# Head of a routed feed-forward kernel: VectorE's turned squares put behind the choice of the group in front

## The chip, the cores and the metric

One core of a Trainium2 chip runs the whole program. The metric is the device time of one execution in microseconds (us); lower is better. The engines' short names are those of the profile: PE is TensorE (PEld its weight loads), DVE is VectorE, ACT is ScalarE, POOL is GpSimd, and SP is SyncE, which here issues nearly all plain DMAs. The "q" of SPq marks an instruction that an engine's sequencer runs, such as the issue of a DMA.

## What is computed

A causal convolution of seven taps per head is followed by a feed-forward layer in which each row goes to one of eight experts, by the largest logit.

```python
# x (8, 3584, 192); weight (8, 7): softmax over the taps, heads of 24 columns
out = einsum('hk,bskhg->bshg', w, x_unf)          # convolution; then 28672 rows of 192
logits = x @ w_gate + modality_bias[modality_id]  # 8 experts
e_idx = argmax(logits, axis=1)
gate_w = softmax(logits)[arange(N), e_idx]
for e in range(8):
    h = maximum(x[e_idx == e] @ w1[e], 0)         # w1 (8, 192, 1024)
    out[e_idx == e] = gate_w * (h @ w2[e])        # w2 (8, 1024, 192)
```

## The kernel before

The rows go through in 19 groups (`QUADS_OF_GROUP` = 1, 1, 2, 1, 1, 2, then 4 each; the code counts them from 0). A quad is four tiles of 120 rows of four batches. The code's group g goes through these steps.

1. SP loads its input, one DMA of 384 KB for each quad (`load`, L317 and L320). The first eleven groups load into two long-lived tiles, so the load of a later group waits until the convolutions of an earlier one have read the place. In the trace these loads are `x<-in_x_dram`.
2. `convolve_pair` (L365, PE) makes the convolution of two heads in PSUM (`cv`); ACT, and DVE for a few, copies it to the tile `y` (L368, L370).
3. `turn` (L385, DVE) turns the 32x32 squares of `y` for one quad into the tile `turned`: one STREAM_TRANSPOSE of 128x768.
4. `gate` (L405, PE) multiplies `turned` with the gate's weights into `gt`: six matmuls for each quad, which the trace shows as twelve.
5. `logits` (L412, L415, DVE) turns `gt` back and adds the bias. `choose` (L428 to L446, DVE with one exponential on ACT) takes the largest logit (`top`, `ex`, `rk`, `first`) and the one-hot choice `oh` (L441).
6. `place` (L463, L466 on PE; L468 to L487 on DVE) counts the rows of each expert and gives the row numbers `idx` (L487). The running count `carry` goes on to the next group.
7. `send` (L251, POOL) scatters the tiles to their experts' rows in DRAM, one indirect DMA for each tile.

The first four groups (`FIRST` = 4: four, four, eight and four tiles, 20 scatters) make chunk 0. Once its rows are counted, `table(0)` (L634 to L698, DVE) works out which expert each slot of rows belongs to. From the table SP issues slot 0's weights (L736, L738, L741) and, behind the landing of chunk 0's scatters, the slot's rows (`raw<-routed_rows`, L771) and `tags`. The code's group 6, of four quads, still runs before slot 0: its four squares are turned, gated and chosen, and behind its gates stand the products `tps` that turn slot 0's rows (L802 to L804). Then comes the long part of the program: matmuls L835, L855 and L859 over 38 slots, into which the later groups are mixed.

Within the head (everything ahead of the first L835) nothing fixes the order by hand: a scheduler places each engine's instructions once, when the program is built, and each engine then runs its own queue in that order. `tc.issue_after(ins)` tells the scheduler to put what is recorded under it behind `ins`. SP's queue is such a list too, so an instruction of SP that waits holds back every DMA behind it.

Of the kernel before, what the change touches and what calls it, by code (L numbers as in the profile page):

```python
# [14 lines left out]
ALU = mybir.AluOpType  # L15
# [34 lines left out]
def conv_then_routed_ffn(ctx, tc, x, weight, modality, w_gate, mod_bias, w1, w2, out):  # L50
    nc = tc.nc
    NB, S, D = x.shape
# [11 lines left out]
    OVER = 2  # L64
    Q = 32
    NK = D // Q
    W = D + OVER
# [21 lines left out]
    turns, state = {}, {}  # L89

    def ring(pool, n, shape, dtype, name, tag=None):

        tag = tag or name
        k = turns[tag] = turns.get(tag, -1) + 1
        return pool.tile(shape, dtype, name=name, tag=f"{tag}_{k % n}", bufs=1)
# [25 lines left out]
    def warm(n):  # L121
# [9 lines left out]
        out=tri, in_=ones, compare_op=ALU.is_gt, fill=0.0, base=0,  # L131
# [145 lines left out]
    class Group:  # L277
# [103 lines left out]
        def turn(self, q):  # L381

            t0 = self.b0 + 4 * q % NB
            self.turned = ring(gp, 2, [P, NK, 4, Q], F32, "turned")
            nc.vector.transpose(out=self.turned.rearrange("p k t c -> p t k c"),  # L385
                                in_=self.ys[4 * q // NB][:, t0:t0 + 4, OVER:W].rearrange("p t (k c) -> p t k c", c=Q))

        def part_turned(self, q):

# [29 lines left out]
        def choose(self):  # L419

            n = self.tiles
            lg = self.lg

            def per_tile(ap):
                return ap.unsqueeze(2).broadcast_to([MB, n, E])

            top = rt.tile([MB, NT], F32, name="top")[:, 0:n]
            nc.vector.tensor_reduce(out=top, in_=lg, axis=AX.X, op=ALU.max)  # L428
            ex = rt.tile([MB, NT, E], F32, name="ex", bufs=1)[:, 0:n]
            nc.vector.tensor_tensor(out=ex, in0=lg, in1=per_tile(top), op=ALU.subtract)  # L430
            self.oh_and_none = rt.tile([MB, NT, E], BF16, name="oh")[:, 0:n + (self.g < SUMMED)]
            self.oh = self.oh_and_none[:, 0:n]
            if self.g < SUMMED:
                nc.vector.memset(self.oh_and_none[:, n], 0.0)
            rk = rt.tile([MB, NT, E], F32, name="rk", bufs=1)[:, 0:n]
            nc.vector.scalar_tensor_tensor(out=rk, in0=ex, scalar=0.0, in1=ramp.unsqueeze(1).broadcast_to([MB, n, E]),
                                           op0=ALU.is_equal, op1=ALU.mult)
            state["exp"] = nc.scalar.activation(out=lg, in_=ex, func=AF.Exp).ins
            first = rt.tile([MB, NT], F32, name="first")[:, 0:n]
            nc.vector.tensor_reduce(out=first, in_=rk, axis=AX.X, op=ALU.max)  # L440
            nc.vector.tensor_tensor(out=self.oh, in0=rk, in1=per_tile(first), op=ALU.is_equal)  # L441
            den = rt.tile([MB, NT], F32, name="den")[:, 0:n]
            nc.vector.tensor_reduce(out=den, in_=lg, axis=AX.X, op=ALU.add)
            nc.vector.tensor_scalar(out=den, in0=den, scalar1=1e-9, scalar2=None, op0=ALU.add)
            for i, y in enumerate(self.ys):
                nc.vector.reciprocal(out=y[0:MB, self.b0:self.b0 + self.nb, 0], in_=den[:, i * self.nb:(i + 1) * self.nb])  # L446
                with tc.issue_after(state["scatter"]) if "scatter" in state else nullcontext():
                    nc.gpsimd.iota(y.bitcast(I32)[0:MB, self.b0:self.b0 + self.nb, 1], pattern=[[S, self.nb]],
                                   base=self.b0 * S + (self.block + i) * MB - CUT + MB - 1,
                                   channel_multiplier=-1)  # L450
# [47 lines left out]
    FIRST = GROUPS_OF_CHUNK[0]  # L498
# [583 lines left out]
```

## Time and profile before

| | us |
|---|---|
| median of 3 runs | 1234.53 (1234.31 to 1235.81) |
| the profiled execution's own time | 1234.43 |
| its span, first to last instruction | 1232.6 |
| what lies around the span | 1.8 |
| PE busy in the span | 1211.1 (98%) |
| DVE busy | 967.9 (79%) |
| ACT busy | 723.3 (59%) |
| POOL busy | 528.7 (43%) |
| PE's first matmul of slot 0 (L835) | starts at 56.68 |

Times in the trace are counted from the span's start. A row of a timeline gives start, length, engine, line, operation, output and input; the brackets at its end give the engine's idle time just before, and what ended it. The chain of waits lists, in order of time, the pieces of work that led to the end.

### The profile page before, as it was taken

The numbers are of one execution on the slowest core, as the hardware profiler recorded it, in microseconds if no ns is written. First come the engines' busy times: TensorE is split into PE (matmuls) and PEld (weight loads), VectorE is DVE, ScalarE is ACT, GpSimd is POOL, SyncE is SP. The second block draws the span as 40 slices with busy tenths as digits, with TensorE's granted clock in tenths as the row PEclk, the third lists the DMA queues.
The fourth block names the chain that finished last, engine by engine and source line by source line (L and its number), as shares of the span: only waits on it lengthen the run. The fifth ranks groups of instructions, "written<-read, shape, count | busy, mean of one in ns | idle before, by whom it ended". The sixth has DMA issues, their size and how long they took to land.

```text
span 1232.6 us, 27980 instructions
## 1 busy us (share of the span) xinstructions
PE 1211.1 (98%) x9220; PEld 1196.6 (97%) x9220; DVE 967.9 (79%) x2455; ACT 723.3 (59%) x1588; POOL 528.7 (43%) x549
## 2 busy tenths in 40 slices
PE   9899999999999999999999999999999999999996
PEld 7799999999999999999999999999999999999995
DVE  6788986888788888788778887777766666787894
ACT  2366655565666556666655666555555555566773
POOL 7756564636344343545445344344352122112221
PEclk9999999999999999999999999999999999999998
DMA  8897563345544354345532554233262344943271
GB/s 222 221 224 211 122 179 77 77 116 142 134 88 111 84 125 110 72 107 142 143 63 57 109 121 126 53 71 61 73 158 56 81 106 106 258 112 94 42 191 38
DMA packets 308448, 144.29 MB, mean 117 GB/s; under 512 B 222922, under 2 KB 294930, under 8 KB 308293
## 3 DMA queue, kind: packets, MB, share of 16 engines
q1 hardware_dynamic: 284574, 97.83, 36.7%
q0 software_dynamic: 22752, 44.54, 11.6%
q8 instruction: 74, 1.21, 0.4%
q14 instruction: 81, 0.66, 0.2%
q10 hardware_dynamic: 967, 0.03, 0.0%
HBM read 116.58 MB, written 51.82 MB: 137 GB/s over the span
## 4 chain that ended last, share of the span: by engine, by line
PE 84%; DVE 6%; DMA 3%; issue 3%; ACT 1%; POOL 1%; SPq 0%; POOLq 0%; DVEq 0%; ACTq 0%
PE hps L835 39%; PE po L855 25%; PE po L859 12%; PE gt L405 3%; PE cv L349 3%; PE cv L365 2%; DMA routed_rows<-y,idx 1%; DVE hl L839 1%; DVE w1b L110 1%; DMA xr<-in_x_dram 1%; ACT lowp L871 1%; DVE xl L110 1%; DVE w2b L110 1%; POOL out_dram L874 0%; DVE sxs L822 0%
## 5 line engine op out<-in xcount | busy, mean ns | idle before, releaser
L855 PE MATMUL po<-w2b,hh 128*128 128x384 f32 x1824 | 556.3, 355 | 0.0
L835 PE MATMUL hps<-sxh,w1b 128*128 128x256 f32 x1824 | 482.0, 287 | 3.2 <-DVE hl L839 2.0
L839 DVE SCALAR_TENSOR_TENSOR hl<-hps,hh 128x512 fp32r<-128x512 f32 x456 | 312.0, 686 | 193.9 <-ACT hh L838 191.2
L838 ACT ACTIVATE hh<-hps 128x512 fp32r<-128x512 f32 x456 | 272.7, 598 | 324.6 <-PE hps L835 319.1
L859 PE MATMUL po<-w2b,hl 128*128 128x192 f32 x1824 | 443.4, 253 | 0.0
L874 POOL DMA_INDIRECT out_dram<-o,tags x228 | 236.5, 1037 | 382.5 <-DVE o L873 320.3
L251 POOL DMA_INDIRECT routed_rows<-y,idx x240 | 262.3, 1093 | 300.4 <-DVE hl L839 146.8
L835 PE MATMUL hps<-sxs,w1b 128*128 128x256 f32 x1824 | 363.5, 281 | 0.4 <-DVE sxs L822 0.4
L835 PEld LDWEIGHTS hps<-sxh,w1b 128*128 128x128 f32 x1824 | 344.8, 189 | 8.5 <-DVE hl L839 8.0
L859 PEld LDWEIGHTS po<-w2b,hl 128*128 128x128 f32 x1824 | 346.2, 191 | 0.0
L855 PEld LDWEIGHTS po<-w2b,hh 128*128 128x128 f32 x1824 | 344.3, 189 | 0.7 <-DVE o L873 0.4
L835 PEld LDWEIGHTS hps<-sxs,w1b 128*128 128x128 f32 x1824 | 280.0, 189 | 0.7 <-issue 0.7
L835 PE MATMUL hps<-sxl,w1b 128*128 128x256 f32 x912 | 256.3, 281 | 0.0
L835 PEld LDWEIGHTS hps<-sxl,w1b 128*128 128x128 f32 x912 | 173.0, 190 | 0.0
L110 DVE TENSOR_TENSOR w1b<-raw,w1b 128x512 fp32r<-128x512 f32 x152 | 101.3, 676 | 6.2 <-ACT w1b L108 5.9
L871 ACT ACTIVATE lowp<-po,tags 128x192 f32<-128x192 f32 x228 | 83.5, 417 | 30.9 <-PE po L855 30.8
L108 ACT CAST w1b<-raw 128x512 fp32r<-128x512 f32 x152 | 92.8, 621 | 3.4 <-DMA raw<-in_moe_w_dram 2.6
L110 DVE TENSOR_TENSOR w2b<-raw,w2b 128x384 fp32r<-128x384 f32 x152 | 80.9, 542 | 8.0 <-ACT w2b L108 7.6
L873 DVE SCALAR_TENSOR_TENSOR o<-po,tags,lowp 128x192 f32<-128x192 f32 x228 | 84.5, 412 | 2.2 <-ACT lowp L871 2.2
L820 ACT CAST sxs<-tp 64x128 fp32r<-64x128 f32 x224 | 66.7, 298 | 30.1 <-DVE tp L795 27.4
L108 ACT CAST w2b<-raw 128x384 fp32r<-128x384 f32 x152 | 75.9, 512 | 1.1
L822 DVE TENSOR_TENSOR sxs<-tp,sxs 64x128 fp32r<-64x128 f32 x224 | 64.8, 289 | 8.6
(158 smaller groups left out, 966.4 us busy)
## 6 DMA issues: line engine op xcount, KB each, us to landing
raw<-in_moe_w_dram SPq DMA_DIRECT2D x38, 768.0 KB
raw<-in_moe_w_dram SPq DMA_DIRECT2D x38, 512.0 KB
raw<-in_moe_w_dram SPq DMA_DIRECT2D x76, 256.0 KB
near<-routed_rows SPq DMA_DIRECT2D x208, 64.0 KB
xr<-in_x_dram SPq DMA_DIRECT2D x32, 384.0 KB
x<-in_x_dram SPq DMA_DIRECT2D x26, 384.0 KB
routed_rows<-filler SPq DMA_DIRECT2D x9, 776.0 KB
far<-routed_rows SPq DMA_DIRECT2D x208, 32.0 KB
```

The source lines that it names most:

```text
L108: nc.scalar.copy(out=hi, in_=raw)
L110: return nc.vector.tensor_tensor(out=lo, in0=raw, in1=f(hi), op=ALU.subtract).ins
L251: state["scatter"] = nc.gpsimd.indirect_dma_start(out=scr, out_offset=bass.IndirectOffsetOnAxis(ap=idx, axis=0), in_=src, in_offset=None,).ins
L820: nc.scalar.copy(out=hi, in_=raw)
L835: nc.tensor.matmul(hps[:, u, :], wa[:, c, fs], mv[z], start=n == 0, stop=n == len(terms) - 1)
L838: nc.scalar.activation(out=hh, in_=hps, func=AF.Relu)
L839: hl_ins = nc.vector.scalar_tensor_tensor(out=hl, in0=hps, scalar=0.0, in1=f(hh), op0=ALU.max, op1=ALU.subtract)
L855: nc.tensor.matmul(po, hh[:, u, js], wb[:, c, :], start=c == 0, stop=c == NF - 1, skip_group_check=True)
L859: nc.tensor.matmul(po[:, 0:D], hl[:, u, js], wb[:, c, 0:D], start=False, stop=False, skip_group_check=True)
L871: nc.scalar.activation(out=lowp, in_=po[:, D:2 * D], func=AF.Copy, scale=gate)
L873: turn_behind(nc.vector.scalar_tensor_tensor(out=o, in0=po[:, 0:D], scalar=gate, in1=lowp, op0=ALU.mult, op1=ALU.add))
L874: st = nc.gpsimd.indirect_dma_start(out=out, out_offset=bass.IndirectOffsetOnAxis(ap=tag.bitcast(I32)[:, j, 1:2], axis=0), in_=o, in_offse ...
```

## The change

In `turn` the STREAM_TRANSPOSE of the code's groups 1 to 4 (five squares: one, two, one, one) is put behind an instruction of the group in front: the first square of a group behind that group's one-hot choice `oh`, a second square behind its row numbers `idx`. Group 0 and the groups from 5 on have no such order. No instruction is added, removed or resized.

```diff
             self.turned = ring(gp, 2, [P, NK, 4, Q], F32, "turned")
-            nc.vector.transpose(out=self.turned.rearrange("p k t c -> p t k c"),
-                                in_=self.ys[4 * q // NB][:, t0:t0 + 4, OVER:W].rearrange("p t (k c) -> p t k c", c=Q))
+            pin = state["idx" if q else "oh"] if 0 < self.g <= FIRST else None
+            with tc.issue_after(pin) if pin else nullcontext():
+                nc.vector.transpose(out=self.turned.rearrange("p k t c -> p t k c"),
+                                    in_=self.ys[4 * q // NB][:, t0:t0 + 4, OVER:W].rearrange("p t (k c) -> p t k c", c=Q))
...
-            nc.vector.tensor_tensor(out=self.oh, in0=rk, in1=per_tile(first), op=ALU.is_equal)
+            state["oh"] = nc.vector.tensor_tensor(out=self.oh, in0=rk, in1=per_tile(first), op=ALU.is_equal).ins
```

The scheduler answers with other orders on DVE, PE, ACT and SP in the head; POOL's order is the same, and behind the head all orders are the same but for line numbers, which are two higher from L387 on. The first place is DVE's choice for group 0. `turned_359` is group 1's square, `turned_424` and `turned_426` are group 2's. Before:

```order
L428 TENSOR_REDUCE top_306<-lg_293 120x4
L385 STREAM_TRANSPOSE turned_359<-y0_182 128x4x6x32
L430 TENSOR_TENSOR ex_308<-lg_293,top_306 120x32
L436 SCALAR_TENSOR_TENSOR rk_312<-ex_308,ramp_173 120x32
L440 TENSOR_REDUCE first_315<-rk_312 120x4
L443 TENSOR_REDUCE den_318<-lg_293 120x4
L441 TENSOR_TENSOR oh_310<-rk_312,first_315 120x32
L444 TENSOR_SCALAR den_318<-den_318 120x4
L446 RECIPROCAL y0_182<-den_318 120x4
L468 TENSOR_TENSOR carry_331<-rp_333,carry0_175 120x8
```

and of the change:

```order
L430 TENSOR_REDUCE top_306<-lg_293 120x4
L432 TENSOR_TENSOR ex_308<-lg_293,top_306 120x32
L438 SCALAR_TENSOR_TENSOR rk_312<-ex_308,ramp_173 120x32
L442 TENSOR_REDUCE first_315<-rk_312 120x4
L445 TENSOR_REDUCE den_318<-lg_293 120x4
L443 TENSOR_TENSOR oh_310<-rk_312,first_315 120x32
L387 STREAM_TRANSPOSE turned_359<-y0_182 128x4x6x32
L446 TENSOR_SCALAR den_318<-den_318 120x4
L470 TENSOR_TENSOR carry_331<-rp_333,carry0_175 120x8
```

Group 1's square has moved from behind `top` to behind `oh`. The second place is SP's queue around slot 0's weights and rows; `x_767` is the tile of the code's group 7, whose four quads are four loads. Before:

```order
L320 DMA x_767<-in_x_dram 128x4x192 x2
L731 TENSOR_LOAD tab_595
...
L736 DMA raw1_0_85<-in_moe_w1_dram 128x1024
...
L741 DMA raw2_0_87<-in_moe_w2_dram 128x8x192
...
L771 DMA raw2_1_88<-routed_rows 128x2x194
...
L771 DMA tags_639<-routed_rows 128x4x2
L320 DMA x_767<-in_x_dram 128x4x192 x2
```

and of the change:

```order
L320 DMA x_767<-in_x_dram 128x4x192
L733 TENSOR_LOAD tab_595
...
L738 DMA raw1_0_85<-in_moe_w1_dram 128x1024
...
L743 DMA raw2_0_87<-in_moe_w2_dram 128x8x192
...
L773 DMA raw2_1_88<-routed_rows 128x2x194
...
L773 DMA tags_639<-routed_rows 128x4x2
L320 DMA x_767<-in_x_dram 128x4x192 x3
```

The load of group 7's second quad has moved from ahead of the table to behind `tags`. The third place is PE's queue at the end of the head, with the semaphores waited for: `cv_1112` is the first pair of heads of group 7, `gt_868` and `gt_878` are the gates of group 6's third and fourth square. Before:

```order
L405 MATMUL gt_856<-turned_834,wg_whole_215 128x128 x5
L365 MATMUL cv_1112<-x_767,band_202 120x192 [waits DMAHW7_49,DMAHW0_49,DVE_49]
L365 MATMUL cv_1112<-x_767,band_202 120x192
L405 MATMUL gt_868<-turned_854,wg_whole_215 128x128 [waits DVE_49]
...
L802 MATMUL tps_906<-ident_95,raw2_1_88 128x128 [waits DMASW2_49,DMAHW5_49,DMASW1_49,DMASW0_49]
```

and of the change:

```order
L407 MATMUL gt_856<-turned_834,wg_whole_215 128x128 x5
L365 MATMUL cv_1112<-x_767,band_202 120x192 [waits DMAHW7_49,DVE_49]
L365 MATMUL cv_1112<-x_767,band_202 120x192
L407 MATMUL gt_868<-turned_854,wg_whole_215 128x128 [waits DVE_49]
...
L804 MATMUL tps_906<-ident_95,raw2_1_88 128x128 [waits DMASW2_49,DMAHW4_49,DMASW1_49,DMASW0_49]
```

Here nothing has moved. `cv_1112` reads the first two quads of `x_767`; the two DMAs raised two semaphores (7 and 0) before, and both raise semaphore 7 now.

## Rows read from the trace of the kernel before

**Rows 1.** The page's part 1: busy us of each engine, share, instructions.

```profile
PE 1211.1 (98%) x9220; PEld 1196.6 (97%) x9220; DVE 967.9 (79%) x2455; ACT 723.3 (59%) x1588; POOL 528.7 (43%) x549
```

**Rows 2.** The chain of waits, where slot 0's matmuls begin to run on.

```profile
64.68 1.21 PE hps L835 x8
```

**Rows 3.** PE's timeline at the end of the head: start, us, what.

```profile
36.72 0.18 PE L463 MATMUL rp<-oh,tri 120*120 120x40 bf16 x1 [1.87 <-DVE oh L441]
...
37.71 4.58 PE L405 MATMUL gt<-turned,wg_whole 128*128 128x128 f32 x24 [0.60 <-DVE den L444]
...
49.51 2.95 PE L405 MATMUL gt<-turned,wg_whole 128*128 128x128 f32 x24 [0.84 <-ACT y L368]
52.29 0.81 PE L365 MATMUL cv<-x,band 128*120 128x192 f32 x4
52.94 2.84 PE L405 MATMUL gt<-turned,wg_whole 128*128 128x128 f32 x24
55.61 0.38 PE L802 MATMUL tps<-ident,raw 128*128 128x128 f32 x2
```

**Rows 4.** ACT's timeline, 46 to 49 us.

```profile
46.70 0.62 ACT L108 CAST w1b<-raw 128x512 fp32r<-128x512 f32 x1 [1.25 <-DMA raw<-in_moe_w_dram]
...
48.97 0.48 ACT L368 COPY y<-cv 120x384 f32<-120x384 f32 x1 [0.76 <-DMA routed_rows<-y,idx]
```

**Rows 5.** POOL's timeline: the first and the last of chunk 0's 20 scatters.

```profile
21.54 1.10 POOL L251 DMA_INDIRECT routed_rows<-y,idx  x1 [3.10 <-ACT lg L438]
...
46.88 0.99 POOL L251 DMA_INDIRECT routed_rows<-y,idx  x1 [0.30 <-issue]
```

**Rows 6.** DVE's timeline: the choice of group 0, and two rows of group 1's.

```profile
16.95 0.19 DVE L428 TENSOR_REDUCE top<-lg 120x4 f32<-120x32 f32 x1
17.05 0.97 DVE L385 STREAM_TRANSPOSE turned<-y 128x768 f32<-128x768 f32 x1
...
18.74 0.19 DVE L441 TENSOR_TENSOR oh<-rk,first 120x32 bf16<-120x32 f32 x1
...
19.41 0.17 DVE L468 TENSOR_TENSOR carry<-rp,carry 120x8 f32<-120x8 f32 x1 [0.18 <-PE rp L466]
...
20.18 0.32 DVE L412 STREAM_TRANSPOSE lt<-gt 128x128 f32<-128x128 f32 x1
20.42 0.13 DVE L487 CAST idx<-row 120x4 int32<-120x4 f32 x1
...
20.76 0.18 DVE L428 TENSOR_REDUCE top<-lg 120x4 f32<-120x32 f32 x1
...
21.65 0.19 DVE L441 TENSOR_TENSOR oh<-rk,first 120x32 bf16<-120x32 f32 x1
```

**Rows 7.** SP's timeline, 33 to 62 us: the DMAs that it issues.

```profile
34.89 0.98 SPq L320 DMA_DIRECT2D x<-in_x_dram  x2
...
50.98 0.97 SPq L771 DMA_DIRECT2D raw<-routed_rows  x2
52.15 0.37 SPq L771 DMA_DIRECT2D tags<-routed_rows  x1
52.57 1.10 SPq L320 DMA_DIRECT2D x<-in_x_dram  x2
```

**Rows 8.** The chain of waits: pieces that are a DMA, from issue to landing.

```profile
4.85 2.26 DMA tap_lines<-raw
...
313.45 4.42 DMA xr<-in_x_dram
...
604.86 4.28 DMA xr<-in_x_dram
```

**Rows 9.** Busy us by stretch, with PE's granted clock (PEclk, 1.00 is full).

```profile
38.00:40.00 2.00, 2.00 (x14) 2.00 (x14) 1.27 (x4) 0.00 (x0) 1.59 (x2) 0.66 1.12 381
40.00:42.00 2.00, 2.00 (x12) 2.00 (x11) 0.43 (x3) 0.00 (x0) 1.49 (x2) 0.50 1.02 249
42.00:44.00 2.00, 2.00 (x14) 2.00 (x14) 1.51 (x8) 0.74 (x2) 1.65 (x3) 0.99 1.01 249
```

## The prediction, made before the changed kernel ran

> **What bounds the kernel now.** I read the busy shares first: PE works for 1211.1 of 1232.6 us [rows 1], so time can be lost or won only where PE stands idle, and the change reaches nothing but the head, the time until slot 0's matmuls run on without a break, at 64.68 [rows 2]. PE's timeline there comes next [rows 3]. From 49.51 it runs without a gap through group 6's first two squares' gates, group 7's first convolution pair at 52.29 and the gates of the third and fourth square, up to the products `tps` at 55.61; what begins late in this stretch makes slot 0 late. The stretch began after 0.84 us of waiting for ACT's copy at 48.97, and that copy waited 0.76 us for scatters of rows whose place it reuses [rows 4]. The scatters leave POOL one behind the other: the first at 21.54, the twentieth at 46.88 [rows 5]. So the end of the head hangs on how early POOL's stream starts, and on everything that PE's queue needs between 49.51 and 55.61.
>
> **Group 0's choice comes earlier.** With the square of 0.97 us between them, group 0's `top` and `oh` start 1.79 us apart (16.95 and 18.74); group 1's, with no square between, 0.89 us apart (20.76 and 21.65) [rows 6]. So group 0's `oh` starts 0.90 us earlier, at 17.84. The square then follows it and ends near 18.9, which is what `carry` now waits for: 18.95 for 19.41, 0.46 us gained. The transposition `lt` of group 1 no longer stands in front of `idx` (20.18 to 20.42 [rows 6]), which gives 0.24 more. Row numbers and first scatter come 0.70 us earlier, at about 20.84. POOL has no idle time between its scatters beyond the 0.30 of issue [rows 5] and its order is unchanged, so the twentieth moves by as much. Bounds: 0 if the first scatter's start does not hang on `idx`, 0.90 if all of `oh`'s gain arrives. I take 0.70.
>
> **The other squares come later.** Groups 1 to 4 are now turned behind the choice in front, so each group's gates, choice and count are put in series. By the same durations I estimate group 3's count, the table and slot 0's weights to come about 0.5 us later, and group 5's choice about 1 us. ACT's cast at 46.70 waits for those weights [rows 4] and stands ahead of the copies that group 6's squares are made from, so the start at 49.51 may be anything from 0.7 us earlier to, if all five squares came on the path, 5 x 0.97 = 4.9 us later; I take 0.3 later, with the second square's gates ending at about 52.6 instead of 52.3. At nearly all of these values the next term hides it.
>
> **A load falls behind a long wait.** This carries the sum. SP issued group 7's first two quads at 34.89, ahead of the table and weights, and the other two at 52.57, behind `raw` and `tags` [rows 7]. In the changed order the second quad's load stands in the latter place. SP's queue is in order: `raw` waits at 50.98 for the landing of the last scatters of chunk 0, and the load is queued behind that wait. Nothing on SP is waiting for the load itself, but PE is: the convolution pair at 52.29 reads both quads, and behind it in PE's queue stand the gates of two squares and `tps`, so slot 0 as a whole. In the kernel before that pair did not wait at all [rows 3]. The load's issue is 52.57 less the 0.70 of the scatters: 51.87 (bounds 51.67 and 52.57). For its landing the nearest rows are two later input loads of the same size from the same line, 4.42 and 4.28 us after issue [rows 8]; the shortest DMA of the chain, a tiny one, took 2.26. I take 4.28, since here too other transfers are queued in front (`raw` and `tags`). Landing: 56.15. The pair starts 56.15 - 52.29 = 3.86 us later, and with it everything behind. The weights, which lose this load in front of them, and `raw`, may land a little earlier; nobody can use it before the load is there.
>
> The Trainium skill says of this, in "DMA: Bandwidth & Descriptors", section "Anatomy of one DMA", that a transfer costs about 2.0 us plus its bytes at 436 GB/s, a fit made for GpSimd's path. By that estimate 384 KB land after 2.9 us, at 54.8, and this term would be 2.5 us instead of 3.86. Rows 8 show more for the same size in this kernel.
>
> **PE's clock.** Before 37.71 PE had idled 1.87 and 0.60 us [rows 3]; shortly after it resumed, the granted clock went to half (0.66 over 38 to 40, 0.50 over 40 to 42) and was back at 0.99 over 42 to 44 [rows 9]. These are the levels 1.2 and 2.4 GHz. The 24 gate matmuls there took 4.58 us, against 2.84 for the 24 at 52.94 [rows 3]: 1.74 us lost. In the changed kernel PE idles some 3.5 us in one piece (52.6 to 56.15), more than the 2.47 that came before that fall, so I expect a second fall, which costs 1.74 if PE has work through all of it and less if part of it lies in the idle time. I take 1.5; bounds 0 and 3.5 (two such stretches).
>
> "TensorE: Matmul & The Clock Gate", section "Part 1: The HAM clock gate", of the Trainium skill says that half rate is the default and that activity releases the full one. By that rule the wait is paid twice, and the one fall of this head agrees with it; against a wait that is paid once it makes 1.5 us of difference.
>
> **The sum.** The profiled execution took 1234.43 (span 1232.6 and 1.8 around it), 0.1 under the median. The pair's 3.86 contains the 0.70 gained and hides the 0.3. 1234.43 + 3.86 + 1.5 = 1239.8. Nothing takes it back later: behind the gates DVE, ACT and PE work in a fixed order on what these gates deliver, and at 98% PE has no idle time to give.
>
> **Rivals.**
>
> *The wait without the fall.* PE's idle time comes as one piece but may end before the clock reacts, as the 0.84 us at 49.51 did without any effect on the clock. 1234.43 + 3.86 = 1238.3. For it: one fall in one trace is little to go by. Against it: that fall followed less idle time.
>
> *A short wait.* If the load finds the DMA engines nearly free and lands like the shortest row, 2.26 us after issue, it lands at 54.13: 1.84 us late, 1236.3 without a fall. Against it stand both input loads of rows 8. By the Trainium skill's fit above this case would take 1236.9.
>
> *The load is hidden and the earlier scatters count: not slower.* If the load landed before PE reaches the pair at 52.3 to 52.6, the 0.76 us that ACT waited for scatters would be all that changes: 1234.43 - 0.7 = 1233.7. It decides at a landing within 0.7 us of the issue; the shortest row is three times that. Or SP is not held at 50.98, because the scatters land over 3 us sooner; with the same number of scatters at the same spacing I see no reason.
>
> *The series of squares is the longer path.* With all five squares on the path, the second square's gates end at 52.3 + 4.9 = 57.2, after the load, and the sum is 1234.43 + 4.9 = 1239.3, up to 1241 with a fall. It speaks against this that the squares of groups 3 and 4 have slack: POOL needs their row numbers only 20 us after the first.
>
> *The order is not followed.* DVE, PE and SP run the queue they are given; the change cannot be without effect on the places shown.
>
> **How the numbers follow.** Forecast, wait and fall: 0.60, 1239.8 (its own range 1238.8 to 1241). Wait without a fall: 0.20, 1238.3. Short wait: 0.09, 1236.3 to 1237. Hidden: 0.04, 1233.7. Series of squares, or two falls (1234.43 + 3.86 + 3.5 = 1241.8): 0.07. The top of the range: issue at 52.57 and 4.42 to land gives 56.99, 4.70 late, and with 1.74 it is 1240.9; two falls carry it to 1241.8. At the bottom the short wait is taken in from its middle. Range 1236.6 to 1241.8. About 0.2%, 2.5 us, is what a measurement of this kernel can tell from no change, so slower begins at 1237.0: forecast, no fall, the longer series and a little of the short wait, 0.88. Within 0.2%: most of the short wait and the hidden load, 0.11. Faster needs under 1232.1, for which no step has a price: 0.01.
>
> **What would show it.** In the profile of the changed kernel: SP issues one input load before the weights and three behind `tags`, the first of them near 51.9; POOL's first scatter starts near 20.8; PE idles 3 to 4 us in front of the convolution pair that stands between the two runs of 24 gate matmuls, and the pair starts near 56; the granted clock falls to 0.5 soon after; `tps` starts at 60.5 to 61.5. The load's term is wrong if that pair starts within 1 us of the gates in front of it; the clock's term if PEclk stays at 1.00 there; the statement that nothing is given back, if `tps` is later by more than the total is.

## The result: 9 us slower, and where they arose

The changed kernel takes 1244.01 us (median of 6, 1242.12 to 1245.01), the kernel before beside it 1234.74 (1233.14 to 1237.47): ratio 1.0071, 95% interval 1.0057 to 1.0085, so 7.0 to 10.5 us slower. The forecast of 1239.8 had sign, place and chain right; the size was too small, and the time lies 2.2 us above its range.

PE's busy time hardly moved from [rows 1] (page, part 1):

```profile
PE 1213.9 (98%) x9220; PEld 1199.2 (97%) x9220; DVE 970.2 (78%) x2455; ACT 724.0 (58%) x1588; POOL 528.9 (43%) x549
```

The span grew by 8.4 us (1232.6 to 1241.0), PE's work by 2.8. So some 5.6 us are new idle time, and the rest is the same work, which ran longer. PE's timeline at the end of the head answers to [rows 3] (start, us, what; in brackets the idle time just before and what ended it):

```profile
51.04 2.92 PE L407 MATMUL gt<-turned,wg_whole 128*128 128x128 f32 x24 [0.20 <-DVE turned L387]
58.91 1.61 PE L365 MATMUL cv<-x,band 128*120 128x192 f32 x4 [4.95 <-DMA x<-in_x_dram]
60.31 4.48 PE L407 MATMUL gt<-turned,wg_whole 128*128 128x128 f32 x24
64.63 0.38 PE L804 MATMUL tps<-ident,raw 128*128 128x128 f32 x2
```

Before, the pair `cv<-x` stood at 52.29 without a wait. Now PE idles 4.95 us for its load, the pair starts 6.62 us later, and the 24 gates behind it take 4.48 us instead of 2.84. `tps` starts 9.02 us later: 6.62 by the pair's later start and 2.40 by slower work. Of the 6.62, 1.53 come from the first 24 gates, which start at 51.04 instead of 49.51; without the load's wait, as e5 below shows, `tps` is 2.21 later. The stretches around it (columns as in [rows 9]) show why the work is slower:

```profile
54.00:56.00 2.00, 0.00 (x0) 0.00 (x0) 1.97 (x5) 0.00 (x0) 1.48 (x2) 1.00 0.84 240
56.00:58.00 2.00, 0.00 (x0) 0.00 (x0) 0.08 (x1) 0.00 (x0) 1.60 (x2) 0.73 0.93 264
58.00:60.00 2.00, 1.09 (x4) 1.12 (x5) 0.00 (x0) 0.00 (x0) 1.39 (x3) 0.50 1.09 355
60.00:62.00 2.00, 2.00 (x10) 2.00 (x9) 0.00 (x0) 0.00 (x0) 1.70 (x2) 0.50 1.05 399
62.00:64.00 2.00, 2.00 (x13) 2.00 (x12) 0.51 (x2) 0.00 (x0) 1.52 (x4) 0.57 1.03 301
```

The granted clock falls to half (1.2 GHz) while PE stands idle and stays there until about 63.7 (0.57 over the last two us is half for 1.7 of them). SP's timeline says why the load is late, against [rows 7]:

```profile
37.35 0.37 SPq L320 DMA_DIRECT2D x<-in_x_dram  x1
39.73 0.37 SPq L738 DMA_DIRECT2D raw<-in_moe_w_dram  x1
...
52.27 0.97 SPq L773 DMA_DIRECT2D raw<-routed_rows  x2
53.43 0.39 SPq L773 DMA_DIRECT2D tags<-routed_rows  x1
53.86 1.86 SPq L320 DMA_DIRECT2D x<-in_x_dram  x3
```

One input load goes ahead of the weights and three behind `tags`, as forecast; the pair needs the first of the three. But `raw` is issued at 52.27, not earlier than the 50.98 of before, although POOL issues its scatters earlier (against [rows 5]):

```profile
20.96 1.10 POOL L251 DMA_INDIRECT routed_rows<-y,idx  x1 [2.54 <-DVE idx L489]
...
46.31 0.99 POOL L251 DMA_INDIRECT routed_rows<-y,idx  x1 [0.30 <-issue]
```

Last, the end of `table(0)` on DVE, first in the kernel before (a row that does not stand ahead), then in the changed one, there with `top` of group 0 to count from:

```profile
36.43 0.14 DVE L687 TENSOR_TENSOR tab<-past,live 1x3 int32<-1x3 f32 x1
```

```profile
16.73 0.18 DVE L430 TENSOR_REDUCE top<-lg 120x4 f32<-120x32 f32 x1
...
38.13 0.14 DVE L689 TENSOR_TENSOR tab<-past,live 1x3 int32<-1x3 f32 x1
```

Counted from `top` (16.95 before), the table ends at 19.48 before and at 21.40 now, 1.92 us later. Counting from `top` matters: among the ten profiles below and these two, one for each kernel, `top` itself starts anywhere from 16.73 to 17.68.

### The profile page after: what moved, and what is told of

It reads as the page before. It is cut to its first block, busy times and chain, and to the rows that moved or that the text cites. A ratio compares the mean times of both kernels' runs of the same rounds, so it can differ in the third digit from the quotient of the medians.

```text
span 1241.0 us, 27978 instructions
## 1 busy us (share of the span) xinstructions
PE 1213.9 (98%) x9220; PEld 1199.2 (97%) x9220; DVE 970.2 (78%) x2455; ACT 724.0 (58%) x1588; POOL 528.9 (43%) x549
## 4 chain that ended last, share of the span: by engine, by line
PE 85%; DVE 5%; DMA 3%; issue 2%; POOL 1%; ACT 1%; SPq 0%; POOLq 0%; DVEq 0%; ACTq 0%
PE hps L837 39%; PE po L857 25%; PE po L861 12%; PE gt L407 4%; PE cv L349 3%; PE cv L365 2%; DMA routed_rows<-y,idx 1%; DVE hl L841 1%; DMA xr<-in_x_dram 1%; DVE w1b L110 1%; DMA raw<-in_moe_w_dram 1%; DVE xl L110 1%; POOL routed_rows L251 1%; ACT lowp L873 1%; DMA near<-routed_rows 0%
```

## The experiments

The theory is that the loss is made where group 7's second-quad load stands behind SP's wait, and then by the clock. Its rival is that DVE's longer chain (later table, weights, gates) makes it. Each ratio is to runs of the kernel before on the same chip (medians 1235.13, 1234.93 and 1235.14 for the three sets). A ratio need not be the quotient of the two medians. "Table" is its last write counted from `top`, "wait" PE's idle time ahead of group 7's pair. Line numbers differ by a few from kernel to kernel, and dots in a diff stand for lines left out.

| kernel | median us | ratio, 95% interval | table | wait | tps at |
|---|---|---|---|---|---|
| before | 1234.74 | | 19.48 | none | 55.61 |
| changed | 1244.01 | 1.0071, 1.0057 to 1.0085 | 21.40 | 4.95 | 64.63 |
| e1, group 4 alone | 1243.52 | 1.0073, 1.0056 to 1.0090 | 18.82 | 5.51 | 63.01 |
| e2, groups 1 to 3 | 1238.61 | 1.0028, 1.0019 to 1.0038 | 23.59 | none | 59.95 |
| e3, pair behind the gates | 1237.59 | 1.0019, 1.0009 to 1.0029 | 21.27 | moved | 59.13 |
| e4, wait filled | 1242.43 | 1.0061, 1.0044 to 1.0078 | 21.40 | filled | 62.86 |
| e5, load from ACT's queue | 1236.47 | 1.0010, 1.0000 to 1.0019 | 21.27 | none | 57.82 |
| e6, last weights behind tags | 1243.59 | 1.0075, 1.0053 to 1.0096 | 21.58 | 5.67 | 65.34 |
| e7, group 1 alone | 1235.16 | 1.0004, 0.9994 to 1.0013 | 19.55 | none | 55.99 |
| e8, before, pair behind the gates | 1234.23 | 0.9991, 0.9982 to 1.0001 | 19.46 | moved | 55.35 |
| e9, e1 with e5's load | 1234.04 | 0.9989, 0.9980 to 0.9999 | 19.03 | none | 54.99 |
| e10, e9 with e8's pair | 1234.16 | 0.9993, 0.9984 to 1.0002 | 18.73 | moved | 55.50 |

### One part of the change alone: group 4

```diff
-            pin = state["idx" if q else "oh"] if 0 < self.g <= FIRST else None
-            with tc.issue_after(pin) if pin else nullcontext():
...
+            with tc.issue_after(state["idx" if q else "oh"]) if self.g == FIRST else nullcontext():
...
```

> Only the square of group 4 (the fifth group) stands behind the choice and the row numbers in front; the squares of groups 1 to 3 go where they were before. Group 7's second-quad load stands behind tags, as in the changed kernel; group 0's choice and the first scatter are not moved. Theory (the load behind SP's wait, then the clock): the pair cv<-x of group 7 waits 4 to 5 us for its load, PE falls to half clock behind it, and the total is +7 to +9.5 us on before, 1242 to 1244, with the first scatter still at 21.5 us. Rival (the squares of groups 1 to 3 on DVE's chain make the loss, by a later table, later weights and later gates): at most +3 us, 1235 to 1238.

Group 0's choice, the first scatters and the squares of groups 1 to 3 are as before, the table even ends 0.66 us earlier than before, and still nearly all of the loss is there (8.4 us by the medians, against 9.3). The wait, 5.51 us, is a little longer than the 4 to 5 expected. PE's timeline:

```profile
57.70 1.60 PE L365 MATMUL cv<-x,band 128*120 128x192 f32 x4 [5.51 <-DMA x<-in_x_dram]
59.10 4.07 PE L405 MATMUL gt<-turned,wg_whole 128*128 128x128 f32 x24
63.01 0.38 PE L802 MATMUL tps<-ident,raw 128*128 128x128 f32 x2
```

So a later table is not needed for the loss; the load's place is enough. All four loads of group 7 go into the tile that groups 3 to 5 are convolved from and wait for group 5's last pair. How many of them stand ahead of the table in SP's queue is settled by the scheduler when the program is built: two before, one in e1 and in the changed kernel, four in e2. By which of its rules stays open.

### The other part alone: groups 1 to 3

```diff
-            pin = state["idx" if q else "oh"] if 0 < self.g <= FIRST else None
-            with tc.issue_after(pin) if pin else nullcontext():
...
+            with tc.issue_after(state["idx" if q else "oh"]) if 0 < self.g < FIRST else nullcontext():
...
```

> The squares of groups 1 to 3 stand behind the choice in front, that of group 4 does not. All four loads of group 7's x stand ahead of the table, so none waits behind the rows of slot 0; the choice of group 0 is early, as in the changed kernel. Theory: no idle time of PE ahead of the pair of group 7, no second stretch of half clock, the first scatter near 20.96 us, total within 2.5 us of before (1233 to 1237). Rival (DVE's chain makes the loss): table later by over 1 us as in the changed kernel, total +5 us or more, over 1239.

Here the theory was too simple. The pair does not wait, but the kernel is 3.5 us slower all the same. DVE's timeline: two squares of group 5 now stand ahead of the table's last steps.

```profile
36.27 0.96 DVE L385 STREAM_TRANSPOSE turned<-y 128x768 f32<-128x768 f32 x1
37.29 0.95 DVE L385 STREAM_TRANSPOSE turned<-y 128x768 f32<-128x768 f32 x1
...
40.41 0.14 DVE L687 TENSOR_TENSOR tab<-past,live 1x3 int32<-1x3 f32 x1
```

The table ends 4.1 us later from `top`, the weights come later, and ACT's cast, in front of the copies that group 6's squares are made from, waits for them (ACT, first in the kernel before, then in e2; then PE and a stretch of e2):

```profile
44.07 0.62 ACT L108 CAST w1b<-raw 128x512 fp32r<-128x512 f32 x1 [0.34 <-DMA raw<-in_moe_w_dram]
```

```profile
47.66 0.62 ACT L108 CAST w1b<-raw 128x512 fp32r<-128x512 f32 x1 [3.63 <-DMA raw<-in_moe_w_dram]
```

```profile
52.35 4.44 PE L405 MATMUL gt<-turned,wg_whole 128*128 128x128 f32 x24
```

```profile
52.00:54.00 2.00, 2.00 (x10) 2.00 (x10) 2.00 (x4) 1.43 (x4) 1.70 (x2) 0.50 0.34 99
```

The four input loads in front do not hold the weights up: this cast starts 5.34 us behind the issue of the slot's first weights (42.32), where it started 5.80 behind it before (44.07 less 38.27). The gates start 2.84 us later than the 49.51 of [rows 3] and fall into a stretch of half clock, which was not expected here. So a later table is a second way to lose time. How the five squares act is not the sum of their parts: the table moves by -0.66 with the one of group 4, by +4.1 with the four of groups 1 to 3 and by +1.9 with all five.

### PE not exposed to the load

```diff
-GATED = {2: 1, 3: 1, 4: 2, 5: 3, 6: 5}
+GATED = {2: 1, 3: 1, 4: 2, 5: 3, 6: 5, 7: 6}
```

> The changed kernel with the first convolution pair of group 7 put behind all gates of group 6 (the list that already does so for groups 2 to 6): SP's order, the load behind tags and DVE's order of choices stay as in the changed kernel. Theory: PE no longer stands 4.95 us; the gates end near 57, the products tps start when the slot's rows land (raw issued at 52.3 plus 3 to 4 us, so 56 to 57.5 where they stood at 64.6), no second stretch of half clock; total +1 to +2.5 us on before, 1235.5 to 1237.5. Rival (the rows of slot 0 or the weights are late as well, so the wait only changes its name): tps at 60 or later, total 1239 or more.

> The kernel before with only the first pair of group 7 put behind the gates of group 6: the control for the same edit on the changed kernel. Theory (the pair's place costs nothing by itself where its load is early): within 1.5 us of before, 1233.5 to 1236.5, so that the 2.5 us that stayed with that edit on the changed kernel are the later table and weights. Rival (the pair's place itself costs 2 to 3 us): 1237 to 1238.5.

On the kernel before, the edit is free (0.9991). On the changed kernel it takes 6.4 us of the loss away by the medians and leaves 2.5. `tps` comes later than expected, at 59.13 instead of 56 to 57.5, since the gates start late and, against the expectation, run partly at half clock (PE and a stretch, in e3; the same block of 48 took 5.82 us in e8):

```profile
52.01 7.29 PE L405 MATMUL gt<-turned,wg_whole 128*128 128x128 f32 x48 [0.20 <-DVE turned L385]
```

```profile
52.00:54.00 2.00, 1.99 (x10) 2.00 (x11) 2.00 (x4) 1.40 (x4) 1.43 (x3) 0.55 0.21 57
```

### The load taken out of SP's queue

```diff
-                ld = nc.sync.dma_start(out=xr, in_=x[b0:b0 + 4, s0 - HALO:s0 + MB, :]...)
+                ld = (nc.scalar if (self.g, q) == (7, 1) else nc.sync).dma_start(out=xr, in_=...)
```

> The changed kernel with group 7's second-quad load issued from ScalarE's queue (behind the fourth copy of the group in front) in place of SP's, so that it no longer stands behind SP's wait for the scatters; all else in order as in the changed kernel. Theory: the load lands before 50 us, no standing of PE ahead of the pair, no second stretch of half clock or a short one; what stays is the later start of group 6's gates (51 to 52 against 49.5 in the kernel before) and the later rows; tps at 57 to 59.5, total +1.5 to +3.5 us on before (1236.5 to 1238.5), as with the pair behind the gates. Rival (the load lands late wherever it is issued, since the weights fill the DMA engines): standing of 3 us or more stays, total over 1240.

This leaves everything of the change in place but the load's place behind SP's wait: in the trace DVE, ACT, PE and POOL run the same instructions in the same order as in the changed kernel. The load goes out at 38.30, and PE runs through (ACT's queue, then PE):

```profile
38.30 0.40 ACTq L320 DMA_DIRECT2D x<-in_x_dram  x1
```

```profile
51.41 2.92 PE L405 MATMUL gt<-turned,wg_whole 128*128 128x128 f32 x24 [0.19 <-DVE turned L385]
54.17 0.91 PE L365 MATMUL cv<-x,band 128*120 128x192 f32 x4
55.03 2.94 PE L405 MATMUL gt<-turned,wg_whole 128*128 128x128 f32 x24
57.82 0.38 PE L802 MATMUL tps<-ident,raw 128*128 128x128 f32 x2
```

1236.47 against the changed kernel's 1244.01: 7.5 of the 9.3 us hang on that one place. The 1.5 that stay over the before beside it (interval 0 to 2.4, so hardly clear of no change) go with the later gates: 51.41 against 49.51, of which `top` itself makes 0.71 (17.66 against 16.95).

One thing more differs between the two profiles. The changed kernel has an earlier stretch of half clock too, as the kernel before has [rows 9]; e5 has none, although PE idled as long ahead of the same gates. PE's timeline, the changed kernel, then e5:

```profile
39.31 2.47 PE L407 MATMUL gt<-turned,wg_whole 128*128 128x128 f32 x12 [1.99 <-DVE turned L387]
```

```profile
40.12 1.60 PE L405 MATMUL gt<-turned,wg_whole 128*128 128x128 f32 x12 [1.99 <-DVE turned L385]
```

The stretches behind, in the same order:

```profile
40.00:42.00 2.00, 2.00 (x14) 2.00 (x12) 0.97 (x6) 0.00 (x0) 1.68 (x3) 0.50 1.08 203
```

```profile
40.00:42.00 2.00, 1.83 (x17) 1.75 (x17) 1.83 (x9) 0.00 (x0) 1.39 (x3) 1.00 0.94 308
```

What that is worth was not measured; group 6's gates start 0.56 us earlier in e5, counted from `top` (33.75 for 34.31). The pair e1 and e9 below is free of it: both have that stretch.

### The clock's price alone

The changed kernel with 22 small bf16 products, which nobody reads, between the first 24 gates and the pair, so that PE works while the load is on its way.

```diff
...
+            if cur.g == 6 and t == 3:
+                with tc.issue_after(state["gates", 6]):
+                    warm(22)
+                with tc.issue_after(state["warm"]):
+                    after.convolve(0)
...
```

> The changed kernel with 22 products of the start-up kind (ones by ones, bf16, 480 columns, into a bank that nobody reads) between the first 24 gates of group 6 and the pair of group 7; they fill about 4.4 of the 4.95 us in which PE stood. The pair starts as late as in the changed kernel (58.5 to 59.5). Theory (the standing time brings the half clock, worth 2.4 us): no half-clock stretch behind the pair, gates behind it 2.84 us long instead of 4.48, total 2 to 2.7 us below the changed kernel, 1241.3 to 1242. Rival (half clock follows from something else, or costs nothing beyond the wait): total as the changed kernel, 1243.5 to 1244.5.

```profile
54.15 4.76 PE L125 MATMUL hps<-ones 120*120 120x480 bf16 x22
59.47 0.88 PE L365 MATMUL cv<-x,band 128*120 128x192 f32 x4 [0.55 <-DMA x<-in_x_dram]
60.18 2.84 PE L406 MATMUL gt<-turned,wg_whole 128*128 128x128 f32 x24
62.86 0.38 PE L809 MATMUL tps<-ident,raw 128*128 128x128 f32 x2
```

```profile
58.00:60.00 2.00, 1.45 (x8) 0.88 (x7) 0.00 (x0) 0.00 (x0) 1.70 (x2) 1.00 1.08 346
```

The pair comes as late as in the changed kernel (0.56 us later, with `top` 0.37 later), and the clock does not fall: from the pair to `tps` it takes 3.39 us, against 5.72 in the changed kernel, 2.33 less. So the idle time brings the fall, and in place it costs 2.3 to 2.4. In the totals 1.6 us of it are seen (1242.43), less than the 2 to 2.7 expected; the two intervals overlap, so the total alone does not show it; the trace does.

### What holds up the rows

```diff
             self.load_second = load_second
-            load_second()
+            if i:
+                load_second()
...
             state["load"] = ld
+            if first:
+                with tc.issue_after(ld):
+                    self.load_second()
```

> The changed kernel with the last weights load of slot 0 (768 KB) issued behind tags in place of ahead of the slot's rows. Measures what holds up the issue of the slot's rows. Theory (the scatters' bytes land behind the weights on the same DMA engines, so the rows are issued by the weights' time and not by the scatters' own): the rows are issued 1.5 us or more earlier than in the changed kernel (52.27), near 50.5, with the scatters issued as before. Rival (the scatters' own issue or landing sets it): rows within 0.5 us of 52.27. The total says little, since the weights of the second product then come late: 1240 to 1247.

With slot 0's last weights load (768 KB) out of the way, SP issues the rows 2.19 us earlier than in the changed kernel, though the last scatter left POOL at 46.70, 0.39 later (SP's timeline):

```profile
50.08 0.99 SPq L772 DMA_DIRECT2D raw<-routed_rows  x2
51.27 0.38 SPq L772 DMA_DIRECT2D tags<-routed_rows  x1
```

The stretches show the DMA engines' share (last column but one), first the changed kernel, then e6:

```profile
46.00:48.00 2.00, 1.96 (x19) 1.76 (x18) 1.49 (x9) 1.46 (x4) 1.38 (x4) 1.00 1.09 264
48.00:50.00 2.00, 1.66 (x11) 1.35 (x9) 0.92 (x4) 1.11 (x3) 1.70 (x2) 1.00 1.03 346
```

```profile
46.00:48.00 2.00, 1.96 (x18) 1.77 (x18) 1.49 (x10) 1.82 (x5) 1.54 (x3) 1.00 0.57 168
48.00:50.00 2.00, 1.99 (x13) 1.68 (x11) 1.20 (x4) 0.85 (x2) 1.53 (x2) 1.00 0.36 98
```

In the changed kernel the engines are full up to 50, when the last scatters have long been issued; in e6 they are not. The scatters land behind the weights, and so the rows go by the weights' time, which goes by the table's. The other profiles bear it out: in ten of them SP issues the rows 9.8 to 10.7 us behind the last weights load, but anywhere from 2.9 to 6.0 us behind the last scatter's start; e2 alone, with 8.5 and 6.2, lies aside. The Trainium skill says in "DMA: Bandwidth & Descriptors", section "Issuing engines are not separate DMA queues", that transfers of all issuing engines run interleaved on the same 16 DMA engines; by that rule the weights from SP hold up the scatters from GpSimd, and these runs agree. The total says little, as expected: the pair waited 5.67 us, since the load now stood behind these weights.

### The earlier scatters alone, and the better parts together

```diff
-            pin = state["idx" if q else "oh"] if 0 < self.g <= FIRST else None
-            with tc.issue_after(pin) if pin else nullcontext():
...
+            with tc.issue_after(state["idx" if q else "oh"]) if self.g == 1 else nullcontext():
...
```

> Only the square of group 1 stands behind group 0's choice. SP's order is that of before (group 7's second quad ahead of the table), the first scatter is early as in the changed kernel. Theory (an earlier scatter buys nothing, since the table and the weights set the head, and the load behind SP's wait made the loss): first scatter near 21.0, table's end within 0.6 us of before (36.4), total within 2.5 us of before, 1233 to 1237. Rival (each square that is put behind a choice costs DVE's chain its own share): table 1 us later, total 1238 or more.

Table and SP's order are those of before, and the first scatter is early by DVE's chain: it starts 4.10 us behind `top` (21.37 less 17.27) where it started 4.59 behind it before (21.54 less 16.95). No gain can be seen from it: 1.0004, 0.9994 to 1.0013.

e9 joins e1's single square with e5's load, e10 adds e8's edit.

> The kernel with the square of group 4 alone behind the choice and the row numbers in front, and group 7's second-quad load issued from ScalarE's queue. Of the two effects seen so far (the load behind SP's wait, and the end of the table) the first is taken away, and the second goes the other way: with that one square pinned, the table ended 0.65 us earlier, counted from group 0's logits, than in the kernel before. Theory (these two are all that the change does to the time): no standing ahead of the pair, tps at 54.5 to 56, total 0 to 1.5 us below before (1233.5 to 1235). Rival (something else in the pinned order costs time): 1236.5 or more.

> As the run before it, with the first pair of group 7 behind the gates of group 6 too. Theory: the gates run as one block of 48 and the products tps start as early or up to 0.5 us earlier; total 0 to 1.5 us below before (1233 to 1235). Rival: 1236.5 or more.

PE's timeline of e9:

```profile
48.88 2.94 PE L405 MATMUL gt<-turned,wg_whole 128*128 128x128 f32 x24 [0.84 <-ACT y L368]
51.66 0.81 PE L365 MATMUL cv<-x,band 128*120 128x192 f32 x4
52.31 2.84 PE L405 MATMUL gt<-turned,wg_whole 128*128 128x128 f32 x24
54.99 0.38 PE L802 MATMUL tps<-ident,raw 128*128 128x128 f32 x2
```

The gates start 0.63 us earlier than before, and the total is 1.1 us below it, with an interval that ends just short of no change. It is the one kernel below before by its interval, and among ten kernels that is little to go by; e10 is not told apart from it. The `tps` of e10 is not earlier in its profile, as expected, but 0.51 later; counted from `top` it is 0.20 earlier. That the same square, which cost 8.4 us with the load behind SP's wait, now costs nothing confirms the place of the loss: e1 and e9 run the same order on DVE, ACT, PE and POOL and differ by the queue of one load.

## Why the prediction was right in kind and too small

The forecast put `tps` 5.36 us later (3.86 for the load and 1.5 for the clock); it is 9.02. Of the 3.66 between them, 1.99 are the load's issue, 0.77 its landing and 0.90 the clock.

**Group 0's choice: right, somewhat smaller.** `idx` comes 3.07 us behind `top` (19.80 less 16.73) where it came 3.47 behind it, so 0.40 gained instead of 0.70. The first scatter's 0.58 (21.54 to 20.96) includes 0.22 by which `top` itself was earlier in that profile. By e7 the gain buys nothing.

**The other squares come later: the first term that failed.** The table was put 0.5 us later; it is 1.92, and group 6's gates start 1.53 later instead of 0.3. That the load's wait hides this is right for the gates. But the sum took SP's wait for the scatters to be independent of the weights, and e6 shows that it is not.

**The load behind the wait: right place, wrong issue.** Forecast was an issue at 51.87, the 52.57 of [rows 7] less the scatters' 0.70. It was issued at 53.86, 1.99 us later. Subtracting the scatters' gain was the mistake: their issue did move by 0.57, but what SP waits for is their landing, and they land behind weights that were issued 1.46 us later (39.73 for 38.27). So the load's issue came 1.29 us later than in [rows 7], where 0.70 earlier was forecast. The landing came 5.05 us after issue, with the pair, instead of the 4.28 taken from [rows 8], 0.77 more; e1 has 5.40 (52.30 to 57.70). With the 3.86 of the forecast, 1.99 and 0.77 make the 6.62 measured. The estimate from the Trainium skill's fit ("DMA: Bandwidth & Descriptors", section "Anatomy of one DMA"), 2.9 us for 384 KB, was further off than the rows: that fit has no term for transfers in front, and here `raw`, `tags` and scatters were.

**The clock: right in kind, 1.5 for 2.40.** The price was scaled from a fall that met PE's gates before. This one lasted longer than that one: 0.50 or little more through 58 to 64, where [rows 9] show one stretch of 0.50 between 0.66 and 0.99. PE worked from 58.91 on, so some 4.8 us of work ran at half speed, which is the 2.40. e4 shows it on its own, 2.33. The upper bound of 3.5 held it; the value taken did not. That a fall would come was read from one earlier fall, and e5 has none there behind the same 1.99 us of idle time, so the argument was weaker than it looked; behind the long waits of the changed kernel, e1 and e6 (4.95 to 5.67 us) the fall is there each time. The wait itself, 4.95 instead of 3.5 us, was longer as well.

**Rivals.** The wait without a fall, the short wait and the hidden load are refuted by the rows above. The series of squares was priced as an alternative to the load; e5 shows that a part of it, some 1.5 us (0 to 2.4), may be there beside it once the load is out of the way, and e2 that it can be the loss by itself. The slack that spoke against it is POOL's; the table, which needs group 3's count, had none and came 1.92 later.

**Nothing is given back: open.** `tps` is 9.02 later, the profiled span 8.4, the median 9.3. By the prediction's sign, 0.6 was given back in the profile; but in e1 the difference is 1.3 the other way (`tps` 7.40 later, span 8.7), in e5 0.8 this way (2.21 and 1.4). What makes it stays open.

## What to carry to other kernels

When an order is changed on one engine, read what the scheduler did with the DMAs on the in-order queues: here one load that slid behind a wait cost 7.5 us, and the instructions that were meant to move cost some 1.5 (0 to 2.4). A queue's wait for small scattered writes ends by what else is on the DMA engines, so do not subtract an earlier issue from a landing without looking at the transfers in front. And an idle time of PE of some us is to be priced with the slower work behind it: 4.95 us of standing brought 2.40 more.

## What the runs showed of the hardware

- In the changed kernel the clock fell during the 4.95 us of idle time itself, and stayed low for some 4.8 us after PE had resumed; 22 small products in that idle time, with the same late load, kept it at full speed throughout (2.84 us instead of 4.48 for the same 24 matmuls).
- A shorter idle time did not decide the clock by its length: the same 1.99 us ahead of the same gates was followed by half clock in the changed kernel (0.50 over 40 to 42) and by full clock in e5 (1.00).
- The head starts up to 0.95 us earlier or later from one profile to the next (`top` from 16.73 to 17.68; 16.73 and 17.66 in the changed kernel and e5, where DVE, ACT, PE and POOL run the same order), so a time in the head is to be counted from an event of its own engine.
- A load moved to another engine's queue need not be a matter of bandwidth: issued from ACT at 38.30 it gained 7.5 us, since SP in the changed kernel stood in a wait until 52.27.
